# Fetching the down-projection weights in five transfers instead of one, in a decode step of attention plus gated feed-forward

## The chip, the core and the metric

The kernel runs on one core of one Trainium2 chip. The metric is the device time of one launch in microseconds (us), as the median of several runs. All data are float32. A lower time is better.

## What is computed

One decode step for two sequences. Attention over the last 4096 cached positions and a gated feed-forward block both start from the same normalised `x`, and their results are added to `x`:

```python
xn   = layernorm(x)                                  # x: [2, 1, 512]
q    = (xn @ wq)                                     # 32 heads of 128
k, v = k_cache[:, :, Sk-4096:], v_cache[:, :, Sk-4096:]   # 8 key/value heads, 4 query heads on each
A    = softmax(q k^T / sqrt(128)) v @ wo             # wo: [4096, 512]
gate, up = xn @ W_gate, xn @ W_up                    # [2, 1, 1792] each
B    = ((gate * (gate > 0)) * up) @ W_down           # W_down: [1792, 512]
out  = x + A + B
```

With two rows of `x` there is little arithmetic on each weight. Nearly everything that the kernel does is to bring 95 MB of weights and cache into SBUF once.

## The kernel before

Every large operand passes through one ring of four SBUF buffers (`ring`, `RING = 4`, line 60). Each buffer has 128 partitions and is filled by a DMA that SP issues. SP issues in program order and stops at the first transfer whose buffer is still in use, so the order of the calls in the code is the order on the DMA queue: the two halves of `wq` (line 106), `w_gate` and `w_up` (lines 194 and 195), then sixteen tiles of 4 MB from the K and V caches (lines 388 to 403), then `w_down` (line 404, tile `wd`), then the two halves of `wo` (lines 431 to 434, tiles `wo0` and `wo1`). `wo1`, the last of all, is cut along its rows into five transfers of 8, 4, 2, 1 and 1 sixteenths, so that the multiplications can begin before all of it is there. Only the small `x` comes over ACT's queue, and at the end SP stores the result, `out`.

What is touched here is `load_down` (line 82). It takes a ring buffer of 128 partitions by 14 by 512 elements. Partition p holds rows 14p to 14p + 13 of `w_down`, which lie one behind the other in HBM, so that a partition's part is one run of 28,672 bytes. One DMA over 128 partitions brings it all (3584 KB).

The end of the program runs so. After the scores of the last of four groups (g = 3), SP issues the last two V tiles, then `wd`, then `wo0` and `wo1`, each when its ring buffer comes free. TensorE (PE) computes softmax and values of the last group (lines 405 and 424 to 427). It multiplies `wd` with the feed-forward activations (`project` in lines 428 and 429, 56 calls of a matmul at line 419, two passes each), spreads the heads (line 430), and multiplies `wo0` and `wo1` (lines 435 and 436), all into one PSUM tile `y_ps`. VectorE (DVE) copies that tile to SBUF (line 438) and SP stores it (line 439). A matmul that is the first to read a transfer waits for that transfer's landing.

A landing is told by a semaphore. The tile framework has eight of these for the DMAs (written DMAHW0 to DMAHW7 in the listings below) and hands them out to the DMAs in turn. A DMA that gets a semaphore whose last user isn't yet known to have landed waits for that user before it is issued.

Of the kernel before, what the change touches and what calls it, by code (L numbers as in the profile page):

```python
# [9 lines left out]
F32 = mybir.dt.float32  # L10
# [10 lines left out]
def kernel(  # L21
# [12 lines left out]
    nc = tc.nc  # L34
    P = 128
    B, _, D = x.shape
# [18 lines left out]
    FB = F // P  # L55
# [4 lines left out]
    ring = ctx.enter_context(tc.tile_pool(name="ring", bufs=RING))  # L60
# [8 lines left out]
    def load(name, src, shape):  # L69
        t = ring.tile(shape, F32, name=name, tag="ring")  # L70
        nc.sync.dma_start(t, src)
        return t
# [6 lines left out]
    def load_ff(w, name):  # L79
        return load(name, w.rearrange("(p k) f -> p k f", p=P), [P, KC, F])  # L80

    def load_down():
        return load("wd", w_down.rearrange("(p k) e -> p k e", p=P), [P, FB, D])

    def load_kv(cache, name, g, a):
        r, b = divmod(g, B)
# [88 lines left out]
    for kc in range(KC):  # L175
        m, k = divmod(kc, 2)
# [9 lines left out]
    for kc in range(KC):  # L186
        for r in range(R):
            for c in range(C):
                n = r * C + c
# [212 lines left out]
    scores(*pend.pop())  # L402
    vin = [load_kv(v_cache, "v", g, a) for a in range(NP)]
    dw = load_down()
    for _ in softmax(g):
        pass
# [61 lines left out]
```

## Time and profile before

| what | value |
|---|---|
| median of 3 runs | 232.33 us (232.28 to 232.66) |
| the profiled execution, its own time | 232.63 us |
| its span, first to last instruction | 230.8 us |
| read from HBM | 94.96 MB |
| busy share of the span: PE, DVE, ACT | 78%, 29%, 21% |
| granted TensorE clock, mean | 0.936 |

The profile is of one execution. A share of the DMA is the mean busy share of the core's 16 DMA engines: 1.00 is all of them moving data, 0.50 as much as eight of them. It is worked out from packets that are counted where they start, so in a short window it can come out some per cent too high or too low, above 1.00 too. No view names the engines one by one. A packet is one run of bytes that one engine moves, for most tiles a whole partition's part, and each engine ends its share of a transfer with a packet of a few bytes that raises the semaphore. "Landed" is when the last of these has come. PEld is TensorE's loading of weights, which runs beside its matmuls. SPq is SP's sequencer, which issues transfers and waits. In the views a matmul counts once for each of its two float32 passes.

### The profile page before, as it was taken

The page shows a single profiled execution, that of the slowest core. Times are in us where ns is not written, and L with a number is a line of the kernel's source. Part 1 is how long each engine was busy: PE and PEld are TensorE (multiplying, and loading weights), DVE is VectorE, ACT ScalarE, POOL GpSimd, SP SyncE. Part 2 cuts the span into 40 slices and gives each one's busy share as a digit, 9 for nine tenths or more (in the row PEclk, how much of TensorE's full clock was granted, in tenths as well). Part 3 has the DMA queues.
Part 4 walks back from the last instruction along what each step waited for, and adds up shares of the span by engine and source line. Part 5 has one row for each costly group of instructions (what it writes and reads, how often), then busy time and mean ns, then how long its engine had stood idle before and what let it go on. Part 6 is the DMA issues. An engine that isn't in the chain of part 4 may idle for free.

```text
span 230.8 us, 4036 instructions
## 1 busy us (share of the span) xinstructions
PE 180.2 (78%) x1828; PEld 109.7 (48%) x1828; DVE 66.3 (29%) x131; ACT 48.3 (21%) x81; POOL 5.4 (2%) x21
## 2 busy tenths in 40 slices
PE   0066961749999889998899699889979964888393
PEld 0031230249666573664483566458456522247281
DVE  0320021014444561441472233158034133010000
ACT  2000100004444551440351243044033102100000
POOL 8000000000000000000000000000000000000000
PEclk9999797697999999999999799999999998899678
DMA  7999999999999999999999999999999999999980
GB/s 273 426 403 443 437 432 411 454 435 415 420 452 426 420 423 450 420 429 420 435 432 430 426 432 426 429 437 426 429 426 440 420 437 435 417 435 420 406 341 35
DMA packets 3964, 95.21 MB, mean 413 GB/s; under 512 B 452, under 2 KB 460, under 8 KB 876
## 3 DMA queue, kind: packets, MB, share of 16 engines
q1 hardware_dynamic: 3900, 94.90, 96.4%
q8 instruction: 14, 0.23, 0.4%
q10 hardware_dynamic: 48, 0.07, 0.1%
q14 instruction: 2, 0.02, 0.0%
HBM read 94.96 MB, written 0.00 MB: 412 GB/s over the span
## 4 chain that ended last, share of the span: by engine, by line
DMA 52%; PE 40%; DVE 4%; issue 1%; SPq 1%; ACT 1%
DMA k<-in_A_k_cache_dram 37%; PE pk L255 21%; DMA wo<-in_A_wo_dram 11%; PE s L268 8%; PE o L332 5%; DMA x<-in_A_x_dram 4%; PE q_ps L190 3%; PE pp L312 1%; PE oa L348 1%; SPq L434 1%; DVE kT L244 1%; DVE pt L313 1%; ACT p L301 1%; DVE on L244 0%; DVE m L277 0%
## 5 line engine op out<-in xcount | busy, mean ns | idle before, releaser
L255 PE MATMUL pk<-ident,k 128*128 128x128 f32 x512 | 68.0, 287 | 6.4 <-DMA k<-in_A_k_cache_dram 6.3
L255 PEld LDWEIGHTS pk<-ident,k 128*128 128x128 f32 x512 | 58.2, 146 | 21.2 <-issue 17.1
L244 DVE COPY kT<-pk 128x512 f32<-128x512 f32 x64 | 44.2, 691 | 52.6 <-PE pk L255 46.7
L244 ACT COPY kT<-pk 128x512 f32<-128x512 f32 x64 | 37.5, 586 | 81.5 <-PE pk L255 81.5
L332 PE MATMUL o<-v,pt 128*32 128x512 f32 x256 | 31.0, 615 | 0.0
L268 PE MATMUL s<-kT,qz 128*32 128x512 f32 x256 | 30.9, 598 | 0.0
L332 PEld LDWEIGHTS o<-v,pt 128*32 128x32 f32 x256 | 11.0, 113 | 14.6 <-issue 9.9
L190 PE MATMUL q_ps<-wq,xnT 128*32 128x512 f32 x64 | 11.9, 914 | 2.8 <-DMA wq<-in_A_wq_dram 2.3
L419 PE MATMUL y_ps<-wo,oT 128*17 128x128 f32 x256 | 10.1, 323 | 5.0 <-DMA wo<-in_A_wo_dram 4.8
L268 PEld LDWEIGHTS s<-kT,qz 128*32 128x32 f32 x256 | 7.0, 109 | 11.9 <-issue 11.5
L348 PE MATMUL oa<-on,pick 128*16 128x128 f32 x64 | 8.3, 273 | 4.1 <-DVE on L244 3.3
L419 PEld LDWEIGHTS y_ps<-wo,oT 128*17 128x17 f32 x256 | 7.9, 116 | 7.0 <-DMA wo<-in_A_wo_dram 6.0
L244 DVE COPY on<-o 128x512 f32<-128x512 f32 x4 | 2.8, 692 | 29.0 <-PE o L332 29.0
L348 PEld LDWEIGHTS oa<-on,pick 128*16 128x16 f32 x64 | 5.8, 97 | 11.1 <-DVE on L244 7.0
L177 PE MATMUL xt_ps<-ident,xn 32*128 32x32 f32 x4 | 1.0, 299 | 12.9 <-DVE xn L172 12.9
L217 PE MATMUL u_ps<-wu,xnT 128*32 128x448 f32 x32 | 4.6, 735 | 6.3 <-DMA wu<-in_B_W_up_dram 6.3
L190 PEld LDWEIGHTS q_ps<-wq,xnT 128*32 128x32 f32 x64 | 2.7, 154 | 11.3 <-issue 7.1
L244 ACT COPY on<-o 128x512 f32<-128x512 f32 x4 | 2.3, 586 | 25.5 <-PE o L332 25.5
L301 ACT ACTIVATE p<-s,nm 128x1024 f32<-128x1024 f32 x4 | 4.5, 1115 | 12.5 <-DVE nm L296 12.5
L177 PEld LDWEIGHTS xt_ps<-ident,xn 32*128 32x128 f32 x4 | 0.8, 206 | 12.8 <-issue 12.8
L312 PE MATMUL pp<-ident,p 128*128 128x128 f32 x32 | 4.9, 279 | 2.4 <-ACT p L301 1.5
L313 DVE TENSOR_TENSOR pt<-pp,own 128x512 f32<-128x512 f32 x8 | 5.4, 690 | 3.4 <-PE pp L312 3.4
(71 smaller groups left out, 61.5 us busy)
## 6 DMA issues: line engine op xcount, KB each, us to landing
k<-in_A_k_cache_dram SPq DMA_DIRECT2D x8, 4096.0 KB, 29.2
v<-in_A_v_cache_dram SPq DMA_DIRECT2D x8, 4096.0 KB, 31.2
wq<-in_A_wq_dram SPq DMA_DIRECT2D x2, 4096.0 KB, 17.5
wo<-in_A_wo_dram SPq DMA_DIRECT2D x1, 4096.0 KB, 31.5
wg<-in_B_W_gate_dram SPq DMA_DIRECT2D x1, 3584.0 KB, 30.2
wu<-in_B_W_up_dram SPq DMA_DIRECT2D x1, 3584.0 KB
wd<-in_B_W_down_dram SPq DMA_DIRECT2D x1, 3584.0 KB, 27.9
wo<-in_A_wo_dram SPq DMA_DIRECT2D x1, 2048.0 KB, 21.6
```

The source lines that it names most:

```text
L190: nc.tensor.matmul(q_ps[r][32 * c:32 * c + 32, :], xnT[:, 0, kc, :], wqt[kc // 2][:, kc % 2, n * 512:(n + 1) * 512], start=(kc == 0), stop ...
L217: nc.tensor.matmul(dst[32 * c:32 * c + 32, :], xnT[:, 1, kc, :], wt[:, kc, c * FQ:(c + 1) * FQ], start=(kc == 0), stop=(kc == KC - 1),)
L244: (nc.vector.tensor_copy if turn[0] % 2 else nc.scalar.copy)(dst, src)
L255: nc.tensor.transpose(pk[:, u * P:(u + 1) * P], kt_in[:, j * P:(j + 1) * P], ident)
L268: nc.tensor.matmul(ss[g][32 * q:32 * q + 32, :], qz[:, g, 32 * n:32 * n + 32], kt[:, h, q * 512:(q + 1) * 512], start=(a == 0 and s1 == 0 ...
L301: nc.scalar.activation(p, both, AF.Exp, bias=nm, scale=SCALE, accum_out=l)
L312: nc.tensor.transpose(pp[:, u], pv[:, lo:lo + P], ident)
L313: nc.vector.tensor_tensor(pts[g][:, jh].rearrange("p n u k -> p u n k"), pp.rearrange("p u (n k) -> p u n k", k=HK), own.rearrange("p h i ...
L332: nc.tensor.matmul(o[32 * q:32 * q + 32, :], pts[g][:, jh, n].rearrange("p u k -> p (u k)"), v[:, lo:lo + 512], start=(s1 == 0 and jh == 0 ...
L348: nc.tensor.matmul(oa[g], pick[:, u, 8 - 8 * a:24 - 8 * a], ons[a][:, u], start=(a == 0 and u == 0), stop=(a == NP - 1 and u == 3),)
L419: nc.tensor.matmul(y_ps[32 * e:32 * e + 17, :], lhsT.rearrange("p b s -> p (b s)")[:, 0:17], w[:, e * P:(e + 1) * P], start=False, stop=stop,)
L434: nc.sync.dma_start(wt[:, j0:j1], wo_rows(r, j0, j1))
```

## The change

The one DMA for `wd` becomes five, issued one behind the other to the same buffer. They bring the same bytes to the same places, each byte once:

```diff
+    PARTS = ((0, 112, 0, FB), (112, 8, 0, FB), (120, 8, 0, 10), (120, 4, 10, FB), (124, 4, 10, FB))
+
     def load_down():
-        return load("wd", w_down.rearrange("(p k) e -> p k e", p=P), [P, FB, D])
+        t = ring.tile([P, FB, D], F32, name="wd", tag="ring")
+        src = w_down.rearrange("(p k) e -> p k e", p=P)
+        for p0, n, k0, k1 in PARTS:
+            nc.sync.dma_start(t[p0:p0 + n, k0:k1], src[p0:p0 + n, k0:k1])
+        return t
```

`PARTS` lists first partition, number of partitions, first row and end row within a partition (`FB` is 14). The first transfer brings partitions 0 to 111 whole, in runs of 28,672 bytes. The second brings partitions 112 to 119 whole. The third brings the first 10 of 14 rows of partitions 120 to 127, in runs of 20,480 bytes. The fourth and fifth bring the other 4 rows of partitions 120 to 123 and of 124 to 127, in runs of 8,192 bytes. The new lines shift all line numbers behind them by 8.

On SP, from the fetch of `w_down` to the store of the result, before:

```order
21 L71 DMA wd<-in_B_W_down_dram 128x7168 [waits DMAHW1_49,PE_49]
22 L434 DMA wo_1674<-in_A_wo_dram 128x8192 [waits DMAHW2_49,PE_49]
23 L434 DMA wo_1740<-in_A_wo_dram 128x4096 [waits DMAHW3_49,PE_49]
24 L434 DMA wo_1740<-in_A_wo_dram 128x2048
25 L434 DMA wo_1740<-in_A_wo_dram 128x1024
26 L434 DMA wo_1740<-in_A_wo_dram 128x512 x2
27 L439 DMA out_dram<-yo 4x2x128 [waits DMAHW4_49,DVE_49]
```

`wo_1674` is the tile `wo0` and `wo_1740` is `wo1`. The same stretch of SP with the change, where they are `wo_1678` and `wo_1744`:

```order
21 L90 DMA wd<-in_B_W_down_dram 112x7168 [waits DMAHW1_49,PE_49]
22 L90 DMA wd<-in_B_W_down_dram 8x7168
23 L90 DMA wd<-in_B_W_down_dram 8x5120
24 L90 DMA wd<-in_B_W_down_dram 4x2048 x2
25 L442 DMA wo_1678<-in_A_wo_dram 128x8192 [waits DMAHW2_49,PE_49]
26 L442 DMA wo_1744<-in_A_wo_dram 128x4096 [waits DMAHW3_49,PE_49]
27 L442 DMA wo_1744<-in_A_wo_dram 128x2048 [waits DMAHW4_49]
28 L442 DMA wo_1744<-in_A_wo_dram 128x1024 [waits DMAHW5_49]
29 L442 DMA wo_1744<-in_A_wo_dram 128x512 [waits DMAHW6_49]
30 L442 DMA wo_1744<-in_A_wo_dram 128x512 [waits DMAHW7_49]
31 L447 DMA out_dram<-yo 4x2x128 [waits DMAHW0_49,DVE_49]
```

Four transfers stand ahead of `wo0` that weren't there, with no wait of their own. The eight semaphores come round four transfers sooner, so the last four pieces of `wo1` and the store now each wait for the semaphore's last user: for the last V tile, and for the first four pieces of `wd`.

On PE, where the matmuls on `wd` begin, before:

```order
372 L419 MATMUL y_ps<-wd,hT 17x128 [waits DMAHW5_49]
373 L419 MATMUL y_ps<-wd,hT 17x128 x55
374 L362 MATMUL op_1664<-osb_1503,spread 128x32 [waits DVE_49]
375 L362 MATMUL op_1664<-osb_1503,spread 128x32 x7
376 L419 MATMUL y_ps<-wo_1674,oT 17x128 [waits DMAHW6_49]
```

And with the change:

```order
372 L427 MATMUL y_ps<-wd,hT 17x128 [waits DMAHW7_49,DMAHW6_49,DMAHW5_49]
373 L427 MATMUL y_ps<-wd,hT 17x128 x39
374 L427 MATMUL y_ps<-wd,hT 17x128 [waits DMAHW1_49,DMAHW0_49]
375 L427 MATMUL y_ps<-wd,hT 17x128 x15
376 L370 MATMUL op_1668<-osb_1503,spread 128x32 [waits DVE_49]
377 L370 MATMUL op_1668<-osb_1503,spread 128x32 x7
378 L427 MATMUL y_ps<-wo_1678,oT 17x128 [waits DMAHW2_49]
```

The order of the matmuls is the same. The first one on `wd` now waits for three landings, and the one on row 10 of 14 for the two others.

## The prediction

> **What bounds the kernel now.** I read the page first, its row of DMA shares and its counts of packets:
>
> ```profile
> DMA  7999999999999999999999999999999999999980
> DMA packets 3964, 95.21 MB, mean 413 GB/s; under 512 B 452, under 2 KB 460, under 8 KB 876
> q1 hardware_dynamic: 3900, 94.90, 96.4%
> q8 instruction: 14, 0.23, 0.4%
> q10 hardware_dynamic: 48, 0.07, 0.1%
> ```
>
> The DMA engines are busy over 90% in every slice between the first and the last two. The kernel is a stream of bytes, and little but fewer bytes or a better use of the engines can shorten it. Then the chain of waits, at its end:
>
> ```profile
> 202.21 24.94 DMA wo<-in_A_wo_dram
> 227.15 0.04 issue
> 227.19 0.46 PE y_ps L419 x8
> 227.68 0.29 DVE yo L438
> ```
>
> The last piece of `wo1` lands at 227.15, and only 8 matmuls, a copy and the store come behind it. Whatever moves that landing moves the end. Then the windows of the last stretch (columns: length, busy time of five engines, clock, DMA share, GB/s):
>
> ```profile
> 206.00:212.00 6.00, 5.58 (x133) 5.10 (x133) 0.71 (x2) 0.00 (x0) 0.00 (x0) 1.00 0.99 426
> 217.00:221.80 4.80, 4.69 (x91) 3.74 (x95) 0.00 (x0) 0.00 (x0) 0.00 (x0) 0.50 0.97 404
> 222.00:225.40 3.40, 3.40 (x134) 3.34 (x128) 0.00 (x0) 0.00 (x0) 0.00 (x0) 1.00 0.70 268
> 223.00:223.50 0.50, 0.50 (x30) 0.49 (x24) 0.00 (x0) 0.00 (x0) 0.00 (x0) 1.00 0.86 340
> 223.50:224.00 0.50, 0.50 (x28) 0.50 (x20) 0.00 (x0) 0.00 (x0) 0.00 (x0) 1.00 0.60 234
> 224.00:224.50 0.50, 0.50 (x28) 0.49 (x24) 0.00 (x0) 0.00 (x0) 0.00 (x0) 1.00 0.55 213
> 224.50:225.00 0.50, 0.50 (x28) 0.47 (x20) 0.00 (x0) 0.00 (x0) 0.00 (x0) 1.00 0.39 156
> 225.00:225.50 0.50, 0.50 (x28) 0.45 (x20) 0.00 (x0) 0.00 (x0) 0.00 (x0) 1.00 0.44 148
> 225.50:226.00 0.50, 0.35 (x17) 0.12 (x8) 0.00 (x0) 0.00 (x0) 0.00 (x0) 1.00 0.33 123
> 226.00:226.40 0.40, 0.40 (x16) 0.23 (x10) 0.00 (x0) 0.00 (x0) 0.00 (x0) 1.00 0.32 118
> 226.40:226.80 0.40, 0.36 (x13) 0.13 (x8) 0.00 (x0) 0.00 (x0) 0.00 (x0) 1.00 0.10 36
> 226.80:228.00 1.20, 0.58 (x16) 0.13 (x8) 0.29 (x1) 0.00 (x0) 0.00 (x0) 1.00 0.00 0
> ```
>
> This is what matters here: the sixteen engines don't end together. Times 16, the shares say that 14 run at 223.0 to 223.5, some 9 or 10 up to 224.5, 6 or 7 up to 225.5, 5 up to 226.4, and none from 226.8. So half of them are out of work by 224.5, the rest up to 2 or 3 us later, though each got the same bytes of every tile. The missing shares from 223.0 to 226.8 add up to 0.5 × (0.14 + 0.40 + 0.45 + 0.61 + 0.56 + 0.67) + 0.4 × (0.68 + 0.90) = 2.05 us of all sixteen. With the work spread evenly all would end at 226.8 − 2.05 = 224.75. That is the most a redistribution could give, 2.05 us.
>
> What holds some engines back can be read from the counts. Queue q8 fetched instructions in 14 packets, 0.4% of 16 × 230.8 us, or 1.06 us each. An engine that gets two of them is at least 2.1 us behind one that gets none. Fourteen fetches as six twos and two ones, on eight engines, fit the steps above (5 or 6 last, 2 or 3 between, the rest early), if one costs an engine about 1.5 us with the change of queue. This is a reading, since no view names the engines.
>
> **The change, step by step.** *The price of a row.* At 206 to 212 us one engine moves 426 / (16 × 0.99) = 26.9 GB/s. A partition's part of `wd`, 28,672 bytes, is 1.07 us of one engine, 20,480 bytes are 0.76, and 8,192 bytes 0.30.
>
> *Who moves the rows.* All transfers of before but two are spread over 128 partitions. The counts show how a transfer is dealt out. Of the 27 tile transfers on SP each has 128 + 16 packets, and 27 × 144 = 3888. The 12 that are left of q1's 3900 are the store of `out`, 8 packets of data and 4 endings: its access pattern begins with a 4 on one side, and it used four engines. `x` has q10's 48, 32 of data and 16 endings. So 112 partitions should go to 16 engines, 7 to each, and 8 or 4 partitions to 8 or 4 engines, one to each (an estimate from these counts). Every engine then gives up one row, −1.07 us. Eight engines get 1.07 + 0.76 back, and four of these 0.30 twice more. Against before, eight engines end 1.07 us earlier, four 0.76 us later, and four 1.07 + 0.76 + 0.61 − 1.07 = 1.37 us later. (8 × 1.07 = 8.5 = 4 × 0.76 + 4 × 1.37, as it must be.)
>
> Which eight is what the traces don't tell. [...]
>
> *The sum.* If the eight that give are the eight with fetches, the last of them ends at 226.8 − 1.07 = 225.7. The early half ends by 224.5 at the latest, plus 1.37 makes 225.9 at the worst, and 223.5 + 1.37 = 224.9 for most. So the last piece lands about 1.07 us earlier, at 226.1. If an engine that ends only near 225.0 is among the four that get 1.37, it ends at 226.4, and the gain is 0.4. The upper end: 1.07, and 0.3 more if an engine runs out before its second fetch comes.
>
> *Can PE follow?* It runs without a gap from 217.1 until shortly before the third piece of `wo1`, at half clock up to 222:
>
> ```profile
> 202.00 3.60 PE L332 MATMUL o<-v,pt 128*32 128x512 f32 x29
> 217.11 8.34 PEld L419 LDWEIGHTS y_ps<-wo,oT 128*17 128x17 f32 x224 [4.69 <-DMA wo<-in_A_wo_dram]
> 225.88 0.35 PEld L419 LDWEIGHTS y_ps<-wo,oT 128*17 128x17 f32 x16 [0.43 <-DMA wo<-in_A_wo_dram]
> 226.55 0.13 PEld L419 LDWEIGHTS y_ps<-wo,oT 128*17 128x17 f32 x8 [0.32 <-DMA wo<-in_A_wo_dram]
> 227.19 0.13 PEld L419 LDWEIGHTS y_ps<-wo,oT 128*17 128x17 f32 x8 [0.51 <-DMA wo<-in_A_wo_dram]
> ```
>
> It is done with all that is there at 225.88 − 0.43 = 225.45, so it isn't far from being the bound itself. With `wo0` 1.07 us earlier, it begins 1.07 us earlier, at 91 / 4.69 = 19 matmuls a microsecond, 21 in all. At full clock (134 / 3.40 = 39 a microsecond) those save 0.5 us, so it is done at 224.9, and the third piece, which let it go on at 225.88, would do so at 224.8. PE is 0.1 late for that one, needs 16 / 39 = 0.4 for it, and waits again for the fourth (226.55 − 1.07 = 225.5) and the fifth. Nothing is lost. A gain much over 1.5 us PE would eat.
>
> *SP.* Four more issues stand ahead of `wo0`:
>
> ```profile
> 179.39 0.34 SPq L71 DMA_DIRECT2D wd<-in_B_W_down_dram  x1
> 185.58 17.06 SPq L434 DMA_DIRECT2D wo<-in_A_wo_dram  x6
> 227.99 0.69 SPq L439 DMA_DIRECT2D out_dram<-yo  x1
> ```
>
> An issue takes 0.34 us, or 0.69 for the store over few engines, so four more take 1.4 to 2.8. `wd`'s then end at 182.5 at the latest, and `wo0` waits until 185.58 for its buffer anyway. Cost nothing; without that cover, up to 2.8 us on SP, and still nothing on the engines, which at 182 are busy with earlier tiles. The new waits of the `wo1` pieces: the second waits for a V tile that PE multiplies from 202 on, the later three for pieces of `wd`, the store for another. `wd` landed at 179.39 + 27.9 = 207.3:
>
> ```profile
> DMA to landing us min/median/max: 27.9/27.9/27.9
> ```
>
> So the last three issues, which were done soon after 202.2, move to about 208. An engine comes to those bytes after all of `wo0` (landed at 217.1), so 9 us of cover are left. PE's second wait in `wd` falls where it had 4.69 us of idle time before `wo0`. Cost nothing.
>
> *The sum against the profile's own time:* 232.63 − 1.07 = 231.56. The median of the runs is 0.30 below the profiled execution, so 232.33 − 1.07 = 231.26, say 231.3.
>
> **The rivals.** *A. The wrong eight.* If fetches go to engines that also get the rows, an engine that ends at 226.8 now ends 0.76 or 1.37 later: 233.1 to 233.7. For it: no row tells the halves apart. [...] I give it 0.08, the number here that has least under it.
>
> *B. A narrow way into SBUF.* [...] I give it 0.12.
>
> [...]
>
> *C. No shift.* The small transfers could be cut finer and spread over all sixteen, or an engine that gets 1.37 ends where the last did, or PE, at half clock for longer, takes back the gain. Then 231.9 to 232.7, most likely 232.3. I give it 0.10.
>
> **How the numbers follow.** The forecast 0.70, A 0.08, B 0.12, C 0.10. About 0.2%, 0.46 us, is what the measurement can tell from no change. The forecast's own range, 0.4 to 1.4 us of gain, is 230.9 to 231.9, with little of it within 0.46. C adds up to 232.7, and both together hold 0.80. Faster 0.70, same 0.10, slower 0.08 + 0.12 = 0.20.
>
> **What would show it.** Right: q1 counts 3900 − 144 + 112 + 16 + 2 × 16 + 2 × 8 = 3932 packets. The DMA share stays near 1 up to about 224 and falls within 2 us, the last piece lands near 226.1, and PE has no idle time left before the third piece and little before the fourth. A: the share falls at the same time or earlier, and a tail of two to four engines reaches past 227. B: GB/s drops well below 426 between 201 and 212, `wd` lands after 210 and PE waits for it. C: the steps of the share stand where they were. The forecast is wrong if `wd` lands later than 207, if SP issues `wo0` later than 186, or if the last landing moves by less than 0.4 us.

## The result, and the profile after the change

| what | before | with the change |
|---|---|---|
| median | 232.31 us (232.28 to 232.66, 4 runs) | 245.09 us (244.13 to 245.91, 4 runs) |
| ratio, 95% interval | | 1.0545 (1.0504 to 1.0586) |
| the profiled execution, its own time | 232.63 us | 244.13 us |
| its span | 230.8 us | 242.3 us |

The change costs 12.8 us in the median. The forecast was 231.3, so it had the sign wrong. The page of the changed kernel, its DMA rows:

```profile
DMA  7999999999999999999999999999999999989980
GB/s 266 437 433 416 450 421 441 433 425 427 430 433 433 433 426 433 425 433 430 427 426 427 433 430 422 427 433 430 433 430 427 433 279 258 179 200 425 392 350 32
DMA packets 3996, 95.21 MB, mean 393 GB/s; under 512 B 476, under 2 KB 484, under 8 KB 900
q1 hardware_dynamic: 3932, 94.90, 96.5%
q8 instruction: 14, 0.23, 0.4%
```

The two upper rows have to be read together. The DMA share stays at 9, but GB/s falls from about 430 to between 179 and 279 in four slices (each is 242.3 / 40 = 6.06 us) and is back at 425 after them. The engines were all busy and moved little. Windows of the changed kernel over that stretch (columns as in the prediction, the last two are DMA share and GB/s):

```profile
190.00:194.00 4.00, 1.78 (x15) 1.54 (x16) 0.73 (x4) 1.21 (x2) 0.00 (x0) 0.76 1.03 442
194.00:198.00 4.00, 3.11 (x24) 0.97 (x26) 1.48 (x4) 0.00 (x0) 0.00 (x0) 0.50 1.10 290
198.00:202.00 4.00, 3.23 (x29) 0.74 (x22) 0.00 (x0) 0.59 (x1) 0.00 (x0) 0.89 1.00 231
202.00:206.00 4.00, 4.00 (x40) 2.30 (x40) 0.00 (x0) 0.00 (x0) 0.00 (x0) 1.00 1.03 276
206.00:210.00 4.00, 1.50 (x13) 0.69 (x8) 1.03 (x2) 0.00 (x0) 0.00 (x0) 1.00 1.14 197
210.00:214.00 4.00, 0.00 (x0) 0.00 (x0) 0.00 (x0) 0.00 (x0) 0.00 (x0) 0.82 0.84 132
214.00:218.00 4.00, 0.00 (x0) 0.00 (x0) 0.00 (x0) 0.00 (x0) 0.00 (x0) 0.50 0.97 246
218.00:222.00 4.00, 2.51 (x48) 2.34 (x52) 0.00 (x0) 0.00 (x0) 0.00 (x0) 0.50 0.94 401
```

Before moved 408, 434, 449, 418 and 430 GB/s in the five windows from 194 to 214, 428 in the mean. From 194 to 218 the changed kernel moved 4 × (290 + 231 + 276 + 197 + 132 + 246) = 5488 KB, which at 428 take 12.8 us and took 24. So 11.2 us are lost here, and the span grew by 11.5 (the profiled execution is the shortest of the four): this stretch is nearly the whole loss. `wd` is what the engines fetch in it. The chain of the changed kernel's end:

```profile
180.31 39.04 DMA wd<-in_B_W_down_dram
219.38 19.44 DMA wo<-in_A_wo_dram
238.85 0.46 PE y_ps L427 x8
239.34 0.29 DVE yo L446
```

`wd` stands on it now, where it did not stand before. Its first transfer, from the page's list of DMA issues (the last figure is us from issue to landing):

```profile
wd<-in_B_W_down_dram SPq DMA_DIRECT2D x1, 3136.0 KB, 38.8
```

And PE's wait for it, from the changed kernel's list of waits (us in total, times, longest):

```profile
PE y_ps L427 <- DMA wd<-in_B_W_down_dram: 11.2, 1, 11.2
```

`wd` landed 27.9 us after its issue before; its 112 partitions alone now need 38.8, and PE waits 11.2 us for them. The trace's packet records say it once more: a row of 28,672 bytes took 1.07 us of its engine before (median of 128), and takes 2.01 now (median of 120), with 3.76 the longest.

### The profile page after: what moved, and what is told of

Same layout as the page of the kernel before. It is cut to its first block, busy times and chain, and to the rows that moved or that the text cites. A ratio compares the mean times of both kernels' runs of the same rounds, so it can differ in the third digit from the quotient of the medians.

```text
span 242.3 us, 4042 instructions
## 1 busy us (share of the span) xinstructions
PE 181.6 (75%) x1828; PEld 112.1 (46%) x1828; DVE 66.5 (27%) x131; ACT 48.3 (20%) x81; POOL 5.4 (2%) x21
## 2 busy tenths in 40 slices
DMA packets 3996, 95.21 MB, mean 393 GB/s; under 512 B 476, under 2 KB 484, under 8 KB 900
## 3 DMA queue, kind: packets, MB, share of 16 engines
q1 hardware_dynamic: 3932, 94.90, 96.5%
## 4 chain that ended last, share of the span: by engine, by line
DMA 64%; PE 32%; DVE 2%; issue 1%; SPq 0%; ACT 0%
DMA k<-in_A_k_cache_dram 36%; PE pk L263 21%; DMA wd<-in_B_W_down_dram 16%; DMA wo<-in_A_wo_dram 8%; PE s L276 6%; DMA x<-in_A_x_dram 4%; PE q_ps L198 2%; PE o L340 1%; DVE kT L252 1%; PE pp L320 0%; SPq L90 0%; DVE stats L163 0%; PE xt_ps L185 0%; PE xt_ps L188 0%; DVE xn L180 0%
## 5 line engine op out<-in xcount | busy, mean ns | idle before, releaser
L263 PEld LDWEIGHTS pk<-ident,k 128*128 128x128 f32 x512 | 58.4, 147 | 20.6 <-issue 16.6
L427 PE MATMUL y_ps<-wd,hT 128*17 128x128 f32 x112 | 4.8, 353 | 11.2 <-DMA wd<-in_B_W_down_dram 11.2
L276 PEld LDWEIGHTS s<-kT,qz 128*32 128x32 f32 x256 | 7.1, 109 | 11.9 <-issue 11.5
L198 PE MATMUL q_ps<-wq,xnT 128*32 128x512 f32 x64 | 9.0, 716 | 4.0 <-DMA wq<-in_A_wq_dram 3.5
L185 PE MATMUL xt_ps<-ident,xn 32*128 32x32 f32 x4 | 1.0, 298 | 12.8 <-DVE xn L180 12.8
L427 PEld LDWEIGHTS y_ps<-wd,hT 128*17 128x17 f32 x112 | 4.3, 128 | 11.7 <-issue 11.4
L320 PE MATMUL pp<-ident,p 128*128 128x128 f32 x32 | 5.7, 316 | 2.4 <-ACT p L309 1.5
L198 PEld LDWEIGHTS q_ps<-wq,xnT 128*32 128x32 f32 x64 | 2.2, 130 | 10.1 <-issue 5.0
## 6 DMA issues: line engine op xcount, KB each, us to landing
wd<-in_B_W_down_dram SPq DMA_DIRECT2D x1, 3136.0 KB, 38.8
```

What stands on the lines that cost most here:

```text
L185: nc.tensor.transpose(xt_ps[:, 0, kc, :], xn.rearrange("r (m p k) -> r m k p", m=2, k=2)[:, m, k], ident[:32, :32])
L198: nc.tensor.matmul(q_ps[r][32 * c:32 * c + 32, :], xnT[:, 0, kc, :], wqt[kc // 2][:, kc % 2, n * 512:(n + 1) * 512], start=(kc == 0), stop ...
L263: nc.tensor.transpose(pk[:, u * P:(u + 1) * P], kt_in[:, j * P:(j + 1) * P], ident)
L276: nc.tensor.matmul(ss[g][32 * q:32 * q + 32, :], qz[:, g, 32 * n:32 * n + 32], kt[:, h, q * 512:(q + 1) * 512], start=(a == 0 and s1 == 0 ...
L320: nc.tensor.transpose(pp[:, u], pv[:, lo:lo + P], ident)
L427: nc.tensor.matmul(y_ps[32 * e:32 * e + 17, :], lhsT.rearrange("p b s -> p (b s)")[:, 0:17], w[:, e * P:(e + 1) * P], start=False, stop=stop,)
```

## The experiments

Two theories stood against each other at first. *W* is the prediction's rival B made wider: the place counts, and rows that several engines write into partitions near each other at once slow each other, in the small transfers and in the first as well. Its word *way* stands for what they would share there; no view shows one. *N* holds that the partitions don't matter: a transfer over few engines costs by itself, and one over 16 costs nothing. Every kernel is `before` with another `load_down`, unless more is shown. Results, each against the kernel before on the same chip:

| run | median us (lowest to highest) | ratio (95%) |
|---|---|---|
| e1_112_16 | 247.23 (247.20 to 247.27) | 1.063 (1.0609 to 1.0651) |
| e2_halves | 243.87 (243.48 to 244.26) | 1.0485 (1.0464 to 1.0506) |
| e5_128_own | 232.52 (232.32 to 234.02) | 1.0005 (0.9991 to 1.002) |
| e6_128_packed | 240.20 (239.37 to 241.03) | 1.0328 (1.0286 to 1.037) |
| e4_112_own | 241.42 (240.90 to 241.95) | 1.0381 (1.0354 to 1.0408) |
| e9_128_two | 237.25 (236.13 to 238.50) | 1.022 (1.0168 to 1.0271) |
| e11_four | 236.79 (236.75 to 236.82) | 1.0188 (1.017 to 1.0207) |
| e7_aligned | 236.36 (236.25 to 236.52) | 1.0164 (1.0149 to 1.0179) |
| e10_layout12 | 236.65 (236.47 to 236.75) | 1.0181 (1.0168 to 1.0195) |
| e12_layout13 | 234.28 (234.21 to 234.70) | 1.0083 (1.007 to 1.0097) |
| e13_eight12 | 233.25 (231.93 to 233.71) | 1.0032 (1.002 to 1.0044) |
| e14_eight13 | 232.35 (231.41 to 232.58) | 0.9991 (0.9982 to 1.0) |

### The same rows to other partitions

The first pair keeps `wd` whole and adds the four small transfers, with the same source rows, into a ring buffer `z` that nobody reads. So 0.46 MB more are moved. In the first, the rows go to every fourth partition from 0 on, in the second to partitions 112 to 127, as in the change.

```diff
+        nc.sync.dma_start(t[0:128], src[0:128])
+        z = ring.tile([P, FB, D], F32, name="z", tag="ring")
+        for p0, n, k0, k1, z0 in ((112, 8, 0, FB, 0), (120, 8, 0, 10, 1), (120, 4, 10, FB, 2), (124, 4, 10, FB, 3)):
+            nc.sync.dma_start(z[z0:4 * n:4, k0:k1], src[p0:p0 + n, k0:k1])      # e5_128_own
+            nc.sync.dma_start(z[p0:p0 + n, k0:k1], src[p0:p0 + n, k0:k1])       # e6_128_packed instead
```

> w_down in one transfer over 128 partitions as before, and behind it the four small transfers of the changed kernel once more, as extra bytes that nobody reads, into another ring buffer at partitions 0, 4, 8 to 28 (and 1, 5, and so on), so that each engine writes where no other engine of the small transfer does. Theory W: each small row goes at nearly full rate; four engines get 2.4 us of extra work and four 1.8. If these are the engines that ended early, they end by 226 and the time stays at 232.3 us; if they are those that ended last, it is 234.1 to 234.7. Rival N: the small transfers cost what they did in the changed kernel, whose GB/s stayed below 280 for the whole of the small rows: at least 5 us, 237 us or more.

> As the kernel with the extra small transfers to spread partitions, but the extra bytes go to partitions 112 to 127 of that other buffer, where the changed kernel puts them. Theory W: the small rows take 9.7 to 12.2 us of four engines, 5.4 to 7.8 us past the old end: 237.7 to 240.1 us, with GB/s near 200 for some 8 us after w_down has landed at about 207. Rival N: the same as with spread partitions, whatever that is.

Windows of e5_128_own:

```profile
202.00:206.00 4.00, 3.27 (x32) 2.09 (x36) 0.00 (x0) 0.59 (x1) 0.00 (x0) 1.00 1.02 430
206.00:210.00 4.00, 3.17 (x66) 2.06 (x59) 1.03 (x2) 0.00 (x0) 0.00 (x0) 1.00 1.00 429
210.00:214.00 4.00, 4.00 (x90) 3.62 (x82) 0.00 (x0) 0.00 (x0) 0.00 (x0) 1.00 1.03 438
```

And of e6_128_packed:

```profile
202.00:206.00 4.00, 3.86 (x39) 2.32 (x40) 0.00 (x0) 0.09 (x1) 0.00 (x0) 1.00 1.27 278
206.00:210.00 4.00, 1.67 (x16) 0.69 (x8) 1.03 (x2) 0.00 (x0) 0.00 (x0) 0.95 0.95 144
210.00:214.00 4.00, 0.77 (x16) 0.65 (x20) 0.00 (x0) 0.00 (x0) 0.00 (x0) 0.50 0.82 182
```

The two differ in nothing but the destination, and the one costs nothing where the other costs 7.7 us. The source rows and the number of transfers are the same, q1 counts 3948 packets in both, so that as many engines took part, and SP issues the small rows at the same time (185.7 and 185.6). So for the small transfers N falls, and so does any cause on the reading side. The buffer `z` takes a place in the ring and puts off the issue of `wo0` from 185.6 to 202 us; as e5_128_own has that too, it costs nothing. The median packet of 20,480 bytes took 0.77 us in the first and 2.13 in the second. e5_128_own settles two more things. The engines that do the small rows had 1.07 + 0.76, four of them 0.61 more, on top of all their former work, and the end did not move: they are among the early ones, as the forecast said. If the changed kernel's small transfers go over the same engines, as the equal counts suggest, rival A is out.

### The same rows, 64 partitions higher

The rows of e5_128_own, moved up by 64 partitions: `z[64 + z0:64 + 4 * n:4, k0:k1]`. q1 counts 3948 packets here too. The author's idea was that each of the eight engines would now write where one other engine's rows go; no view shows which engine writes where. *W2* in the expectation is W with room for two.

> [...] Rival W2, a way is wider than one engine, and only more than two at once are too many: the extra rows go at full rate, 232.3 to 232.6 us.

Windows of e9_128_two:

```profile
202.00:206.00 4.00, 3.23 (x35) 1.98 (x35) 0.00 (x0) 0.59 (x1) 0.00 (x0) 1.00 1.04 288
206.00:210.00 4.00, 2.51 (x22) 1.04 (x13) 1.03 (x2) 0.00 (x0) 0.00 (x0) 1.00 1.09 253
210.00:214.00 4.00, 2.88 (x64) 2.62 (x68) 0.00 (x0) 0.00 (x0) 0.00 (x0) 0.70 0.91 385
```

20,480 bytes take 1.55 us here, twice the 0.77 of e5_128_own, and 8,192 take 0.62 for 0.31, so W2, by which they go at full rate, is out. The same rows cost nothing at 0, 4, 8... and 4.7 us at 64, 68, 72..., and nothing but the destination differs. An engine has 2.44 us of them at most (1.07 + 0.76 + 0.61), and in e5_128_own that moved no end. Doubled, they take it 2.44 more, and as much from one other engine, if it is one that they slow: the end would come 2.4 us later at most. It came 4.7 later (two runs at 236.1, two at 238.4 and 238.5), so more engines than these are slowed, or each by more.

### Who else is held up

In the next one only four engines bring extra rows: q1 counts 3924 = 3900 + 12 rows + 3 × 4 endings. If they slow one other engine each, as the author took it, eight engines have no part in it. `wd` is whole; three extra transfers, unread again, bring four whole rows each to partitions 64, 68, 72, 76 and so on, where e9_128_two had shown rows to be slowed:

```diff
+        nc.sync.dma_start(t, src)
+        z = ring.tile([P, FB, D], F32, name="z", tag="ring")
+        for z0 in range(3):
+            nc.sync.dma_start(z[64 + z0:80:4], src[112 + 4 * z0:116 + 4 * z0])
```

> [...] Theory W as it stands (a crowded way slows only its users): in that stretch, between about 204 and 211, eight engines go at 13.5 GB/s and eight at 26.9, 320 GB/s in all; time 232.3 + 3.2 = 235.5 us. Theory W with a back-up (whoever waits at a crowded way holds up the others too): all sixteen fall to about half, 210 to 240 GB/s, and the time is the same or somewhat more, 235.5 to 237.

Windows of e11_four, of 2 us:

```profile
202.00:204.00 2.00, 1.52 (x16) 1.16 (x20) 0.00 (x0) 0.42 (x1) 0.00 (x0) 1.00 1.24 438
204.00:206.00 2.00, 2.00 (x24) 1.12 (x20) 0.00 (x0) 0.00 (x0) 0.00 (x0) 1.00 1.07 223
206.00:208.00 2.00, 1.17 (x11) 0.25 (x4) 0.69 (x1) 0.00 (x0) 0.00 (x0) 1.00 1.05 215
208.00:210.00 2.00, 0.84 (x8) 0.49 (x6) 0.34 (x1) 0.00 (x0) 0.00 (x0) 1.00 1.01 225
212.00:214.00 2.00, 2.00 (x46) 1.66 (x40) 0.00 (x0) 0.00 (x0) 0.00 (x0) 0.50 0.99 426
```

If only these four and four others ran at half speed, twelve engines' worth would be left: 12 / 16 × 428 = 321. The rate is 215 to 225, half of everything, with all sixteen busy. The packet records show it too: of the 40 packets of `wd`, `wo0` and the extra rows that started between 204 and 209.5 us, none was quick. Those of 28,672 bytes took 2.02 to 2.26 us (1.07 in before), those of 32,768 bytes 2.33 to 2.54 (1.22 in before). So the extra rows of four engines held up all sixteen: 215 to 225 GB/s in place of 428. By what, no view shows.

### The first transfer alone, and halves

In e4_112_own the change's transfer of 112 partitions is kept, and the small rows go where they cost nothing, into `z` as in e5_128_own. The last 16 partitions of `w_down` are left out of the product.

```diff
+        nc.sync.dma_start(t[0:112], src[0:112])
...
-        project(hT[:, k], dw[:, k], False)
+        project(hT[0:112, k], dw[0:112, k], False)
```

> The changed kernel with its small transfers sent to spread partitions of another buffer, each engine alone on its way, so that only the first transfer, 112 partitions, is as in the changed kernel; the last 16 partitions of w_down are left out of the product. Theory W: what is left of the loss is that of the first transfer, which in the changed kernel ran at 290, 231 and 276 GB/s from 194 to 206 us, 4.6 us lost, and some more to 209: 232.3 + 5 = 237 to 238 us. A rival by which the small transfers are all of the loss: 231.3 us.

Windows of e4_112_own:

```profile
194.00:198.00 4.00, 3.11 (x24) 0.88 (x26) 1.29 (x4) 0.00 (x0) 0.00 (x0) 0.50 1.14 307
198.00:214.00 16.00, 9.44 (x72) 3.73 (x64) 1.03 (x2) 0.59 (x1) 0.00 (x0) 0.82 0.98 223
```

It is slower by 8.9 us than before, more than W had given it. From 198 to 214 us the 112 partitions go in at about half rate, 223 GB/s. That was in no case of the prediction: the first transfer costs 8.9 us without the crowd of the small ones, the small ones 7.7 behind a transfer over all 128 partitions (e6_128_packed). Here the small rows were held up too, as the first transfer was still coming in (1.45 us in the median for 20,480 bytes, 0.77 in e5_128_own), so not all of the 8.9 need be its own. In the changed kernel both together cost 12.8 and not 16.6. That a second crowd costs less while all engines stand behind a first would explain it, but isn't shown.

Two other cuts of the same `wd`, into partitions 0 to 63 and 64 to 127, and into 0 to 111 and 112 to 127:

```diff
+        for p0, n, k0, k1 in ((0, 64, 0, FB), (64, 64, 0, FB)):                  # e2_halves
+        for p0, n, k0, k1 in ((0, 112, 0, FB), (112, 16, 0, FB)):                # e1_112_16
+            nc.sync.dma_start(t[p0:p0 + n, k0:k1], src[p0:p0 + n, k0:k1])
```

> w_down in two transfers, partitions 0 to 63 and 64 to 127, whole rows; everything else as before. [...] Rival N (number): what costs is a transfer over few engines or over a number of partitions that isn't a power of two, wherever it goes; 64 partitions go to 16 engines like 128, so nothing changes: 232.3 us.

> w_down in two transfers, partitions 0 to 111 and 112 to 127, whole rows, both over 16 engines, so that no engine gets more bytes than another. [...] Rival N in its form 'few engines': 232.3, for no transfer uses fewer than 16; in its form 'no power of two': 238, the first transfer alone.

A window of e2_halves over the middle of its `wd`:

```profile
202.00:214.00 12.00, 5.53 (x48) 3.02 (x48) 1.03 (x2) 0.00 (x0) 0.00 (x0) 0.95 1.08 229
```

And three of e1_112_16, in the time of its second transfer:

```profile
210.00:214.00 4.00, 0.00 (x0) 0.00 (x0) 0.00 (x0) 0.00 (x0) 0.00 (x0) 0.50 1.06 144
214.00:218.00 4.00, 0.00 (x0) 0.00 (x0) 0.00 (x0) 0.00 (x0) 0.00 (x0) 0.50 1.00 136
218.00:222.00 4.00, 0.00 (x0) 0.00 (x0) 0.00 (x0) 0.00 (x0) 0.00 (x0) 0.50 0.65 139
```

Half of the partitions give about half of the rate: 229 GB/s are measured, where before moved 428. Both transfers go over 16 engines (3916 = 3900 + 16 endings) and 64 is a power of two, so N falls here in both its forms. At 229 GB/s the 3584 KB of `wd` take 16.0 us, at 428 they take 8.6: 7.4 us more. The time, 243.87, is 11.3 above before: the low rate lasts for 24 us and not 16, since the end of the tile before `wd` and the first rows of `wo0` are slowed with it (2.4 to 2.5 us in the median for 32,768 bytes of `wo0`, in place of 1.22).

In e1_112_16 the rate is 136 to 144 GB/s while sixteen engines write 16 partitions, with `wo0` beside them. Its time, 247.23, is 14.7 above before and above both values of N. The first transfer costs 8.9 us in e4_112_own. If the costs add, that leaves some 5.8 for the second; `wo0` is slowed beside it (3.5 to 4.7 us for its rows of 32,768 bytes, 1.22 in before).

### Can the redistribution be had without the crowd?

The forecast's idea was that eight early engines take work from eight late ones. Five tries follow. The first, e7_aligned, brings the last 2 of 14 rows in four transfers of 32 partitions, cut so that each should use eight engines:

```diff
+        nc.sync.dma_start(t[:, 0:12], src[:, 0:12])
+        for p0 in (0, 32, 64, 96):
+            part = bass.AP(
+                tensor=w_down.tensor, offset=w_down.offset + (p0 * FB + 12) * D,
+                ap=[[4 * FB * D, 8], [FB * D, 4], [1, 2 * D]],
+            )
+            nc.sync.dma_start(t[p0:p0 + 32, 12:FB], part)
```

> [...] Four times 16 KB of one engine's work go to the eight engines that ended early, 2 x 16 KB more than they had (1.2 us), and the others have 1.2 us less. [...] Rival W2: 232.3 - 1.2 = 231.1 us, the gain that was forecast.

The others (e10_layout12, e12_layout13, e13_eight12 and e14_eight13, in this order) deal the rows of `w_down` out anew: `M` = 12 (or 13) rows to every partition and `X` = 4 (or 2) more to partitions 0 to 63, in two transfers of 32. The activations are laid out to match, and the product is the same, in 64 (or 60) calls for 56.

```diff
+    M, X = 12, 4                                                                 # e12_layout13: 13, 2
...
+        nc.sync.dma_start(t[:, 0:M], w_down[0:P * M, :].rearrange("(p k) e -> p k e", p=P))
+        for p0 in range(0, HALF, 32):
+            rest = bass.AP(
+                tensor=w_down.tensor, offset=w_down.offset + (P * M + p0 * X) * D,
+                ap=[[4 * X * D, 8], [X * D, 4], [1, X * D]],                      # e13, e14: [[X * D, 8], [8 * X * D, 4], [1, X * D]]
+            )
+            nc.sync.dma_start(t[p0:p0 + 32, M:M + X], rest)
```

> The shift of bytes without a crowded way: the rows of w_down are dealt anew over the partitions, 12 to each of the 128 and 4 more to each of partitions 0 to 63 (the gate and up products, the transposed activations and the projection follow that split, the result is the same). [...] Theory W: the late engines end at 226.8 - 1.2 = 225.6, the early ones at 224.6 to 225.9, so the time is 231.2 to 231.5 us. Rival: that the early engines have no slack, or that the transfers over 32 partitions cost by themselves as the first kernel's small ones did, 232.3 us or more.

> The same with half the shift: 13 rows of w_down to each of the 128 partitions and 2 more to each of partitions 0 to 63, 16 KB or 0.6 us less for the late engines. Theory W: 231.7 us. Rival as for the larger shift: 232.3 us or more.

> As the new deal with 12 rows to each partition and 4 more to partitions 0 to 63, whose packets showed 16 endings for each transfer over 32 partitions, so that sixteen engines had written there and not eight. Here the order of the extra rows in HBM is changed so that the source begins with an 8 (partition 4j + i of 32 takes block 8i + j), and the activations follow. Theory W: eight endings for each of the two transfers (3900 + 64 + 2 x 8 = 3980 packets on the queue), a row at the full 26.9 GB/s, 0.30 us for 8 KB, GB/s near 430 throughout, and the late engines end 1.2 us earlier: 231.2 to 231.6 us. Rival H, a transfer that isn't over all 128 partitions is slow as such unless it is a comb of single partitions: 236 us again. Rival S, the shift gives nothing because something else ends the kernel: 232.3 us.

> The same with 13 rows to each partition and 2 more to partitions 0 to 63, half the shift, 0.6 us. Theory W: 3980 packets, GB/s near 430, 231.7 to 231.9 us. Rival H: 234 us as with the first new deal of this size. Rival S: 232.3 us.

The queue's packets, of e10_layout12:

```profile
q1 hardware_dynamic: 3996, 94.90, 96.3%
```

And of e13_eight12:

```profile
q1 hardware_dynamic: 3980, 94.90, 96.1%
```

Windows of e13_eight12:

```profile
202.00:206.00 4.00, 3.73 (x39) 2.32 (x40) 0.00 (x0) 0.22 (x1) 0.00 (x0) 1.00 1.08 459
206.00:210.00 4.00, 3.17 (x79) 2.25 (x71) 1.03 (x2) 0.00 (x0) 0.00 (x0) 1.00 1.00 428
```

The first three miss for one reason, which the count gives: 3996 = 3900 + 64 rows + 2 × 16 endings, so each transfer went to sixteen engines and not to eight (e7_aligned has 4092 = 3900 + 128 + 4 × 16). A source whose 8 groups of 4 rows lie one behind the other was dealt out like one of 32. Sixteen engines into 32 partitions crowd again, at 240 and 258 GB/s in e10_layout12 from 202 to 210. With the order of the rows in HBM changed (e13, e14), the endings are 2 × 8, and at 459 and 428 GB/s no crowd is left: eight engines into the same partitions run at full speed.

Still these two miss what was expected of them. e13_eight12 is 0.8 us slower than before. e14_eight13 lies near 231.4 in two of eleven runs and at 232.2 to 232.6 in nine. Its profiled execution is one of the two. PE's last weight loads in it (idle time before them in brackets):

```profile
224.87 0.35 PEld L437 LDWEIGHTS y_ps<-wo,oT 128*17 128x17 f32 x16 [0.44 <-DMA wo<-in_A_wo_dram]
225.52 0.13 PEld L437 LDWEIGHTS y_ps<-wo,oT 128*17 128x17 f32 x8 [0.30 <-DMA wo<-in_A_wo_dram]
226.16 0.13 PEld L437 LDWEIGHTS y_ps<-wo,oT 128*17 128x17 f32 x8 [0.50 <-DMA wo<-in_A_wo_dram]
```

The last piece is there 1.0 us earlier than the 227.19 of before, and PE keeps up, as the forecast had it. The end of e13_eight12, for comparison:

```profile
224.50:225.00 0.50, 0.41 (x16) 0.13 (x7) 0.00 (x0) 0.00 (x0) 0.00 (x0) 1.00 0.42 160
225.50:226.00 0.50, 0.50 (x24) 0.50 (x20) 0.00 (x0) 0.00 (x0) 0.00 (x0) 1.00 0.12 49
226.50:227.00 0.50, 0.39 (x16) 0.35 (x16) 0.00 (x0) 0.00 (x0) 0.00 (x0) 1.00 0.13 49
```

Shares of 0.12 and 0.13 are two engines of sixteen. In before some five ended late; here two end later still (before has 0.05 in the last of these windows), and PE starts on the last piece at 227.93 (227.19 in before). Whether they are engines that gave or engines that got no view shows, and why e14's runs fall into two groups is open too. No version beat the kernel before by more than can be measured.

## Why the prediction was wrong, step by step

**The price of a row failed.** "A partition's part of `wd`, 28,672 bytes, is 1.07 us of one engine" is true where the rows are spread as in before and e5_128_own (1.07 in both). The sum took it for every row, wherever it goes. It is 2.01 in the change. The 0.76 for 20,480 bytes became 2.13 into partitions 112 to 127 (e6_128_packed), and 1.55, double, into 64, 68, 72 and so on (e9_128_two).

**The sum left out the first transfer.** "112 partitions should go to 16 engines, 7 to each" gave −1.07 us for every engine. The count fits that dealing, but it runs at 223 GB/s: 8.9 us more in e4_112_own. Why it is slow isn't shown: the trace doesn't tell which rows each engine writes, and so not which engines write near each other at the same time. Nor was the reading side ruled out for this transfer by itself, as no run sent its rows to other partitions. That it loses about half of the rate is shown, that 64 partitions do so too (229 GB/s), and that it bears the mark of e11_four: the V tile's last rows of 32,768 bytes, beside its first ones, took 2.28 to 2.44 us in e4_112_own from 195.5 us on, and 1.22 in before.

**Rival B had the place right.** It was given 0.12. Its signs came as listed: GB/s far below 426 between 201 and 212, `wd` landing after 210, PE waiting. The 9.7 to 12.2 us, and with them the 237.7 to 240.1, that e6_128_packed was expected to show were the author's estimate from a number of rows that share a way, and no run shows that number. What the run showed is 2.13 us for a row of 20,480 bytes in place of 0.77, all engines slowed (278, 144 and 182 GB/s from 202 to 214), and 240.20 us, 7.7 more. The first transfer is slowed as well, by up to 8.9 us in e4_112_own. Hence 245.1.

**A row of before bore on it.** `x`, 64 KB, goes into 32 partitions by sixteen engines (q10: 32 packets and 16 endings), amid `wq`'s stream:

```profile
5.90:8.80 2.90, 0.00 (x0) 0.00 (x0) 1.00 (x4) 0.00 (x0) 0.20 (x2) 1.00 1.01 395
```

395 GB/s in place of 426 are 0.2 us lost. That looks too little for a price on the place. But while e10_layout12 sent rows to 32 partitions over sixteen engines, the core moved 240 and 258 GB/s. At that rate 64 KB take 0.25 to 0.27 us in place of 0.15, so a loss of 0.1 was to be expected if the place counts, and none if it doesn't. Priced that way, the row could not speak against B. It is weak evidence for it: the packet records have 1.23 to 1.44 us for `wq`'s 32,768 bytes beside `x` (1.21 just before), but 84 ns in the median for `x`'s own packets, no more than the 85 of `wo1`'s packets of the same 2,048 bytes.

**Who gives and who gets was right**, so far as the counts and e5_128_own go: 3932 packets, and receivers with 2.4 us to spare. Whether eight late engines then all end 1.07 earlier is another matter, and not shown: e13_eight12 was meant to take 32 KB, 1.2 us at 26.9 GB/s, from one eight to the other, which is the author's estimate, as no view shows who writes which partitions. In it two engines ended later than the last did in before.

**SP and the new waits cost nothing, as forecast,** though the waits moved. SP in the changed kernel:

```profile
179.50 1.76 SPq L90 DMA_DIRECT2D wd<-in_B_W_down_dram  x5
185.69 34.01 SPq L442 DMA_DIRECT2D wo<-in_A_wo_dram  x6
```

Four more issues took 1.76 − 0.34 = 1.4 us, the lower end of 1.4 to 2.8, and `wo0` was issued at 185.69 (185.58 before). The last pieces of `wo1` waited for `wd` until 185.69 + 34.01 = 219.7 where 208 had been forecast, because `wd` was late. PE's first work on `wo0`:

```profile
228.86 6.96 PEld L427 LDWEIGHTS y_ps<-wo,oT 128*17 128x17 f32 x192 [2.73 <-DMA wo<-in_A_wo_dram]
```

That is 9 us after the last issue, so the cover was still there.

## What to carry to other kernels

In this kernel a transfer into SBUF was priced by the partitions that it writes and by how many engines write there, not only by its bytes: one over all 128 partitions, small ones spread to every fourth partition from 0 on (from 64 on they cost 4.7 us), or two over 32 partitions from eight engines each, ran at full rate (428 to 459 GB/s), and 112, 64, 32 or 16 neighbouring partitions over sixteen engines ran at between 0.6 and a third of it (258 to 136), and everything beside them with them. In the profile of this kernel that was a DMA share near 1 with GB/s at half or less; the share alone hid it. And a row that is to speak against a rival should first be priced by that rival.

## What the runs showed of the hardware that was not expected

- The extra rows of four engines, into partitions 64, 68, 72, 76 and so on, halved the rate of all sixteen (e11_four: 215 to 225 GB/s where 321 would be left if only eight had slowed; `wo0`'s packets of 32,768 bytes 2.33 to 2.54 us in place of 1.22).
- 112 of 128 partitions take longer than 128: 35.4 us from issue to landing in e4_112_own, 27.9 for the whole `wd` before.
- 0.46 MB of extra rows cost nothing at the end (e5_128_own, 232.52 against 232.55), though four engines had 2.44 us more to do: they were among those that end early.
- A source whose outer two dimensions follow at one even step was dealt out like one dimension: 32 partitions written as 8 × 4 went to sixteen engines (e7_aligned and e10_layout12, 4092 and 3996 packets), and to eight once the order in HBM was changed (e13_eight12, 3980).
